# A decode step of attention and an MLP on one core: K tiles in pairs, two accumulator banks, and another order of the tail

## The chip, the core and the metric

The kernel runs on one core of one Trainium2 chip. The metric is the device time of one execution in microseconds, the median over runs. TensorE (PE; its weight loads PEld), VectorE (DVE), ScalarE (ACT) and GpSimd (POOL) compute; SyncE (SP) issues the large transfers, which the core's 16 DMA engines carry out in the order of issue.

## The reference, cut to what matters

Four tokens (B = 4) of width 576 go through an attention over a window of a cache and, in parallel, through a small MLP block; both are added to the input.

```python
xn = layernorm(x)                                   # x: 4 x 1 x 576
# A: attention, 32 query heads, 16 KV heads, Dh 128, window W = 2048 of the last keys of 8192
q = (xn @ wq) as 32 heads
k, v = the last 2048 rows of k_cache, v_cache, each KV head used by 2 query heads
A = (softmax(q k^T / sqrt(128)) v) as 4096 @ wo     # wo: 4096 x 576
# B: MLP; the shifts along the sequence leave zeros, since S = 1
x1 = xn + 0                                         # all four shifted groups are zero
B = x1 + gelu(layernorm(x1) @ w3) @ w4              # w3: 576 x 4608, w4: 4608 x 576
out = x + A + B
```

The time goes into moving data: K and V are 32 MB each in bf16, w3 and w4 5 MB each, wq and wo 4.6 MB each. That is 87 MB in all.

## The kernel before, in words

**Tiles.** K and V are read as eight tiles each of 4 MB (128 partitions x 32 KB), in an order K_order of (bp, kq): bp is a pair of batch elements (32 rows of batch and KV head each), kq is a quarter of the window. All go through one SBUF ring with four slots of a tile each; tile n lies in slot n % 4. Behind the four slots and partly over the last two lie wq and w3, later the first half of w4 (w4_e0, 18 rows of 576 per partition, at REST). The attention output weights wo and the second half of w4 (18 rows, in the pieces E1) come last, over slots 0 and 1.

**Transfers.** All of them are issued by SP, in program order, by cache_load (L124), load_run (L113) and load_w4 (L478). SP waits at each until the place in the ring is free: until VectorE has transposed the K tile there, or until TensorE's matmuls have read the V tile there. V0 to V3 come in two transfers of two tiles (64 KB per partition); K0 to K7 and V4 to V7 come one by one.

**K stage.** k_scores(n) (L278) issues the load of K tile n, lets VectorE transpose it in four instructions of 128 x 2048 int32 (L291) into kt tiles, of which there are two, and multiplies by the queries in 32 matmuls (L300). The scores stand in four PSUM banks S0 to S3. bank_max takes their maxima (L276).

**V stage.** From L508 on, TensorE, ScalarE and VectorE run in the order in which the program is written. exponentials(g) turn one bank into EP (L342). pick_rows (L348) turns the exponentials' rows by matmuls into the layout that V needs; ScalarE copies the result to CB (keep_rows, L358). spread_rows(n) (L367) makes the tile X(n) on VectorE in four instructions of 1.2 us (L373). X(n) is masked so that 64 matmuls of 128 x 256 (v_compute, L380) give the sums over V tile n, in the bank O0 (n = 0 to 3) or O1 (n = 4 to 7). X tiles share two buffers with the kt tiles, so X(n+1) takes the buffer of X(n-1). The matmuls of a quarter of a tile wait for the quarter of X alone.

**Heads.** reciprocal_rows (L394) brings 1 / sum to the rows where the heads are. heads_out(bp) (L405) scales the two halves of O. heads_rows (L410) turns them by four matmuls into OX, and heads_pick (L420) masks and sums OX on VectorE into onx, the left operand of the matmuls with wo. heads_out(0) follows v_compute(3), heads_pick(0) follows v_compute(4).

**The sum.** ACC is one PSUM bank: rows 0 to 3 hold columns 0 to 287 of the result, rows 32 to 35 hold columns 288 to 575. It is started with a matmul of zeros (L212), VectorE writes x + xn into it (L268), and acc_matmuls (L431) adds pairs of matmuls (4 x 288 each), one for each half. mlp_out adds rows of w4 in this way: 18 rows of w4_e0 in two halves, one behind v_compute(6), one behind heads_out(1). Then come the 32 rows of wo and the 18 rows of w4's second half. Last, ScalarE copies the one half of ACC and VectorE the other (L563), and the output is stored.

Of the kernel before, what the change touches and what calls it, by code (L numbers as in the profile page):

```python
# [9 lines left out]
ALU = mybir.AluOpType  # L10
AX = mybir.AxisListType
BF16 = mybir.dt.bfloat16
F32 = mybir.dt.float32
# [5 lines left out]
def kernel(  # L19
# [50 lines left out]
    def ap_of(t, offset_elems, dims):  # L70
        a = t[:]
        return bass.AP(a.tensor, a.offset + offset_elems, [list(a.ap[0])] + [list(d) for d in dims])
# [30 lines left out]
    w3_n = D * F // P  # L103
    wo_n = NQ * D // P
    E0_N = NFH * D
    E1 = (10, 6, 2)
    SLOT = [i * TILE for i in range(4)]
    REST = 4 * TILE
    RING = max(SLOT[2] + wq_n + w3_n, REST + E0_N)
# [11 lines left out]

    v_rows = A_v_cache.rearrange("b h s d -> (b h) s d")

    def cache_load(rows, n, count, tiles, paired):  # L124

        bp, kq = K_order[n]
        t = ring[:, SLOT[n % 4]:SLOT[n % 4] + count * TILE]
        lo = Sk - W + kq // 2 * 8 * CK
        src = rows[MT * bp:MT * bp + MT, lo:lo + 8 * CK, :]
        if paired:  # L130
            src = src.rearrange("m (q h c) d -> m q h (c d)", q=4, h=2)
        else:
            src = src.rearrange("m (h q c) d -> m q h (c d)", q=4, h=2)
        src = src[:, :, kq % 2:kq % 2 + count, :]
        load_run(t, src.rearrange("m q h x -> m q (h x)") if count > 1 else src[:, :, 0, :])
        for i in range(count):
            tiles[n + i] = t[:, i * TILE:(i + 1) * TILE].rearrange("p (c d) -> p c d", d=Dh)
# [40 lines left out]
    def z_part(n, dt):  # L178
        a = z_at[0]
        z_at[0] += n * (1 if dt is BF16 else 2)  # L180
        assert z_at[0] <= ZN
        return Z[:, a:a + n] if dt is BF16 else Zf[:, a // 2:a // 2 + n]
# [95 lines left out]
    def k_scores(n):  # L278

        bp, kq = K_order[n]  # L280
        cache_load(k_rows, n, 1, K_tiles, False)
        kn = K_tiles.pop(n)
        if n == 0:
            S.extend(ps_s.tile([P, 512], F32, tag="S", name=f"S{g}") for g in range(4))
        C2 = CK // 2

        kt = [ktp.tile([P, C2, G, 2, 2], BF16, tag="kt", name=f"kt{n}{e}") for e in range(2)]
        for i in range(4):
            e, a = divmod(i, 2)
            c0 = a * C2 // 2  # L290
            nc.vector.transpose(out=ap32(kt[e], c0 * 2 * G, [[2 * G, C2 // 2], [1, 2], [2, G]]),  # L291
                                in_=ap32(kn, c0 * 4 * G + e * G, [[4 * G, C2 // 2], [2 * G, 2], [1, G]]))
            if n > 4 and i == 1:
                bank_max(n - 5)
        for e in range(2):
            for t in range(2):
                y = 2 * e + t
                for m in range(NM):
                    c = 32 * (m % 4)
                    nc.tensor.matmul(out=S[kq][c:c + 32, :].rearrange("p (c q l) -> p c q l", q=4, l=2),  # L300
                                     lhsT=qz[:, bp, m, y, :], rhs=kt[e][:, :, 4 * m:4 * m + 4, :, t],
                                     start=(bp == 0 and m < 4 and y == 0), stop=(bp == 1 and m >= 4 and y == NY - 1),
                                     skip_group_check=True)
# [6 lines left out]
    permf = z_part(2 * 2 * PB, F32).rearrange("p (b s n) -> p b s n", b=2, s=2)  # L310
    osums = [z_part(Dh, F32) for bp in range(2)]
    masked = z_part(NT * 2 * Dh, F32).rearrange("p (t b x e) -> p t b x e", t=NT, b=2, x=XR)
    picked = z_part(NT * 2 * XR, F32)
    gu = z_part(NG2, F32)

    perm_rows = const.tile([P, 2, PB], BF16)
# [24 lines left out]
    def exponentials(g):  # L341
        nc.scalar.activation(out=EP[:, g].rearrange("p q (c l) -> p c q l", l=2),  # L342
                             in_=S[g][:].rearrange("p (c q l) -> p c q l", q=4, l=2),
                             func=ACT.Exp, bias=nb[:], scale=scale, accum_out=sm[:, g:g + 1])

    CPS = {}

    def pick_rows(bp, r, out, keys):  # L348
        for q in range(4):
            nc.tensor.matmul(out=out, lhsT=pick[:, bp, r, 3 - q:3 - q + P], rhs=ap_of(Z, q * 2 * CK, keys),  # L350
                             start=(q == 0), stop=(q == 3), skip_group_check=True)

    def pick_all(bp):
        for r in range(rep):
            CPS[bp, r] = ps_s.tile([P, NG * CK], F32, tag="S", name=f"C{bp}{r}")
            pick_rows(bp, r, CPS[bp, r][:], [[8 * CK, NG // 2], [1, 2 * CK]])

    def keep_rows(bp, g0, g1):  # L358
        for r in range(rep):
            nc.scalar.copy(out=CB[:, bp, g0:g1, :, r],  # L360
                           in_=CPS[bp, r][:, g0 * CK:g1 * CK].rearrange("p (g c) -> p g c", c=CK))
# [43 lines left out]
    def heads_out(bp):  # L405
        for j in range(2):
            rows = slice(PB * j, PB * j + PB)
            nc.scalar.mul(out=osums[bp][rows], in_=O_tiles[bp][rows, Dh * j:Dh * j + Dh], mul=rd_rows[rows, bp:bp + 1])

    def heads_rows(bp):  # L410
        OX = ps_tp.tile([P, NT, 2, Dh], F32, tag="tp", name=f"OX{bp}")
# [8 lines left out]
    def heads_pick(bp, OX):  # L420
        nc.vector.tensor_tensor(out=masked.rearrange("p t b x e -> p (t b) x e"),  # L421
                                in0=OX[:].rearrange("p t b (e x) -> p (t b) x e", x=XR),
                                in1=ap_of(own_d, 0, [[0, NT * 2], [0, XR], [1, ND]]), op=ALU.mult)
        nc.vector.tensor_reduce(out=picked, in_=masked.rearrange("p t b x e -> p (t b x) e"), op=ALU.add, axis=AX.X)  # L424
        nc.vector.tensor_copy(out=ap_of(onx, 2 * bp, [[XR * B, NT], [1, 2], [B, XR]]),  # L425
                              in_=picked.rearrange("p (t b x) -> p t b x", t=NT, b=2))

    def acc_rows(q):
        return slice(32 * q, 32 * q + B)

    def acc_matmuls(lhsT, row):  # L431
        for q in range(2):
            nc.tensor.matmul(out=ACC[acc_rows(q), 0:DH], lhsT=lhsT, rhs=row[:, q * DH:(q + 1) * DH],  # L433
                             start=False, stop=False, skip_group_check=True)

    G_banks = []
# [38 lines left out]
                             skip_group_check=True)  # L475
        nc.scalar.mul(out=gT[:], in_=GT[:], mul=0.5)

    def load_w4(a, e, i0, n):  # L478
        t = ring[:, a:a + n * D]
        nc.sync.dma_start(out=t, in_=w4_src[e, :, i0:i0 + n, :].rearrange("m i n -> m (i n)"))  # L480
        return t.rearrange("p (i n) -> p i n", n=D), e, i0, n


    def mlp_out(t, e, i0, n, a=0, b=None):
        for i in range(a, n if b is None else b):
# [13 lines left out]
    NV = len(K_order)  # L499
    w4_e0 = load_w4(REST, 0, 0, NFH)  # L500
    for n in range(0, 4, 2):
        cache_load(v_rows, n, 2, V_tiles, True)
    bank_max(NG - 1)
    nc.vector.reduce_max(out=nb[:], in_=mx[:], axis=AX.X)
    nc.vector.tensor_scalar_mul(out=nb[:], in0=nb[:], scalar1=-scale)  # L505
# [1 line left out]
    ENGINES = {mybir.EngineType.PE, mybir.EngineType.Activation, mybir.EngineType.DVE}  # L507
    with tc.manual_schedule(engines=ENGINES):  # L508
        exponentials(0)
        exponentials(1)  # L510
        first = ps_s.tile([P, rep, CK], F32, tag="S", name="first")
        for r in range(rep):
            pick_rows(0, r, first[:, r, :], [[1, CK]])
        exponentials(2)
        for r in range(rep):
            nc.scalar.copy(out=CB[:, 0, 0, :, r], in_=first[:, r, :])
        exponentials(3)
        spread_rows(0)
        v_compute(0, 0, CK // 2)
        pick_all(0)  # L520
        keep_rows(0, 1, NG)
        v_compute(0, CK // 2, CK)
        cache_load(v_rows, 4, 1, V_tiles, True)
        spread_rows(1)
        reciprocals()
        nc.scalar.copy(out=spread, in_=bass.AP(fold[:].tensor, fold[:].offset, [list(fold[:].ap[0]), [1, PB], [0, ND]]))
        for n in range(1, NV):
            v_compute(n)
            if n == 1:
                pick_all(1)  # L530
                keep_rows(1, 0, NG)
                reciprocal_rows()
            if n == 3:
                heads_out(0)
            if n + 1 < NV:
                spread_rows(n + 1)
            if n == 4:
                heads_pick(0, heads_rows(0))
                gelu_u()
            if n == 5:  # L540
                gelu_g()
                gelu_T()
            if n + 4 < NV:
                cache_load(v_rows, n + 4, 1, V_tiles, True)
            if n == 5:
                wo_t = load_run(ring[:, 0:wo_n], flat(A_wo, wo_n))
                end, i0 = [], 0
                for n1 in E1:
                    end.append(load_w4(wo_n + i0 * D, 1, i0, n1))
                    i0 += n1  # L550
            if n == 6:
                mlp_out(*w4_e0, 0, NFH // 2)
        heads_out(1)
        mlp_out(*w4_e0, NFH // 2, NFH)
        heads_pick(1, heads_rows(1))
        for x in range(XR):
            acc_matmuls(onx[:, 0, x, :], wo_t[:, x * D:(x + 1) * D])
        for part in end:
            mlp_out(*part)

    fin = const.tile([B, D], out.dtype, name="fin")
    for q, copy in enumerate((nc.scalar.copy, nc.vector.tensor_copy)):
        copy(out=fin[:, q * DH:(q + 1) * DH], in_=ACC[acc_rows(q), 0:DH])  # L563
    nc.scalar.dma_start(out=o2, in_=fin[:])


# [28 lines left out]
```

## Time and profile before

| What | us |
|---|---|
| median of the runs shown | 212.37 |
| runs | 286.46, 212.37, 212.02 |
| the profiled execution's own time | 212.37 |
| its span, first to last instruction | 210.3 |
| TensorE busy | 122.3 |
| VectorE busy | 128.1 |
| ScalarE busy | 14.6 |

The page divides the span in 40 equal slices of 5.26 us. "PEclk" gives the clock that TensorE was granted in each, in tenths of full speed; "DMA" the busy share of the 16 DMA engines. The chain that ended last follows the execution back from its last instruction: at each step to what released it, or to the instruction before it on its engine. A timeline's row gives start and duration of a group of merged instructions, then engine, line, operation, output and inputs, and in brackets how long the engine had been idle and what ended it ("issue" where the profile shows nothing). The time to landing of a transfer counts from its issue. K stands for the stretch to 121 us, V for the stretch from 131 us on.

### The profile page before, as it was taken

The page shows a single profiled execution, that of the slowest core. Times are in us where ns is not written, and L with a number is a line of the kernel's source. Part 1 is how long each engine was busy: PE and PEld are TensorE (multiplying, and loading weights), DVE is VectorE, ACT ScalarE, POOL GpSimd, SP SyncE. Part 2 cuts the span into 40 slices and gives each one's busy share as a digit, 9 for nine tenths or more (in the row PEclk, how much of TensorE's full clock was granted, in tenths as well). Part 3 has the DMA queues.
Part 4 walks back from the last instruction along what each step waited for, and adds up shares of the span by engine and source line. Part 5 has one row for each costly group of instructions (what it writes and reads, how often), then busy time and mean ns, then how long its engine had stood idle before and what let it go on. Part 6 is the DMA issues. An engine that isn't in the chain of part 4 may idle for free.

```text
span 210.3 us, 2423 instructions
## 1 busy us (share of the span) xinstructions
PE 122.3 (58%) x1071; PEld 75.9 (36%) x1071; DVE 128.1 (61%) x119; ACT 14.6 (7%) x40; POOL 3.2 (2%) x11
## 2 busy tenths in 40 slices
PE   1244199053534333333344400999799999799974
PEld 0121011010111111111111100778588889687752
DVE  6922100889898989899998180049935568950020
ACT  4002100000000000000000410020300101000100
POOL 4100000000000000000000000000000000000000
PEclk9999569855555555555555555599999999999999
DMA  7999999999999999999999999999999999999990
GB/s 300 399 452 465 392 427 461 405 430 461 405 430 461 397 411 474 411 424 461 400 501 399 436 424 511 411 411 402 405 418 452 424 418 433 443 425 438 386 378 25
DMA packets 3193, 87.31 MB, mean 415 GB/s; under 512 B 360, under 2 KB 368, under 8 KB 752
## 3 DMA queue, kind: packets, MB, share of 16 engines
q1 hardware_dynamic: 3168, 87.16, 96.6%
q8 instruction: 8, 0.13, 0.3%
q10 hardware_dynamic: 16, 0.01, 0.0%
q14 instruction: 1, 0.01, 0.0%
HBM read 87.17 MB, written 0.00 MB: 415 GB/s over the span
## 4 chain that ended last, share of the span: by engine, by line
DMA 52%; PE 31%; DVE 12%; issue 1%; SPq 1%; ACT 1%; DVEq 0%
DMA ring<-in_A_k_cache_dram 35%; PE O L386 25%; DMA ring<-in_A_v_cache_dram 17%; DVE kt L291 7%; PE ACC L433 4%; DVE X L373 2%; PE C L350 2%; SPq L114 1%; PE OX L416 1%; DVE Z L421 0%; DVE Z L424 0%; DVE Z L461 0%; DVE gg L465 0%; ACT Z L360 0%; DVE Z L460 0%
## 5 line engine op out<-in xcount | busy, mean ns | idle before, releaser
L291 DVE STREAM_TRANSPOSE kt<-ring 128x2048 int32<-128x2048 int32 x32 | 71.4, 2283 | 19.3 <-DMA ring<-in_A_k_cache_dram 19.2
L386 PE MATMUL O<-ring,X 128*128 128x256 bf16 x512 | 59.3, 279 | 10.6 <-DMA ring<-in_A_v_cache_dram 10.6
L300 PE MATMUL S<-kt,Z 128*32 128x512 bf16 x256 | 30.4, 623 | 50.0 <-DVE kt L291 50.0
L386 PEld LDWEIGHTS <-X 128*128 128x128 bf16 x512 | 51.1, 100 | 18.2 <-issue 11.1
L373 DVE TENSOR_TENSOR X<-Z,own 128x1024 int32<-128x1024 int32 x32 | 37.0, 1218 | 25.4 <-ACT Z L360 13.9
L300 PEld LDWEIGHTS <-Z 128*32 128x32 bf16 x256 | 10.2, 128 | 70.5 <-issue 70.5
L448 PE MATMUL G<-ring,ln2T 128*8 128x512 bf16 (+1 forms) x54 | 10.4, 859 | 2.6 <-DMA ring<-in_B_w_dram 2.6
L421 DVE TENSOR_TENSOR Z<-OX,own_d 128x256 f32<-128x256 f32 x2 | 0.8, 424 | 15.8 <-PE OX L416 15.8
L342 ACT ACTIVATE Z<-S,nb 128x512 bf16<-128x512 f32 x4 | 2.8, 700 | 81.0 <-DVE nb L505 81.0
L448 PEld LDWEIGHTS <-ln2T 128*8 128x8 bf16 x54 | 2.0, 98 | 12.3 <-issue 11.4
L229 PE MATMUL qp<-ring,xnT 128*8 128x512 bf16 x36 | 3.8, 578 | 2.3 <-DMA ring<-in_A_wq_dram 1.8
L240 DVE CAST q_rows<-qp 128x256 bf16<-128x256 f32 x4 | 1.5, 418 | 5.6 <-PE qp L229 4.9
L433 PE MATMUL ACC<-ring,gT 128*4 128x288 bf16 x72 | 4.9, 286 | 0.0
L433 PE MATMUL ACC<-ring,onx 128*4 128x288 bf16 x64 | 4.1, 286 | 1.2 <-DVE onx L425 1.2
L563 DVE CAST fin<-ACC 4x288 bf16<-4x288 f32 x1 | 0.4, 449 | 6.8 <-ACT fin L563 6.8
L360 ACT CAST Z<-C 128x384 bf16<-128x384 f32 (+1 forms) x4 | 2.6, 659 | 27.3 <-PE C L350 27.2
L350 PEld LDWEIGHTS <-pick 128*128 128x128 bf16 x24 | 2.4, 109 | 4.8 <-issue 3.3
L276 DVE TENSOR_REDUCE mx<-S 128x1 f32<-128x512 f32 x4 | 2.7, 671 | 2.0 <-PE S L300 2.0
L350 PE MATMUL C<-Z,pick 128*128 128x512 bf16 x16 | 3.8, 379 | 0.0
L196 PEld LDWEIGHTS <-Z 4*128 4x128 bf16 x16 | 0.8, 104 | 8.1 <-DVE Z L171 4.0
L433 PEld LDWEIGHTS <-onx 128*4 128x4 bf16 x64 | 2.7, 85 | 2.5 <-DVE onx L425 1.4
L433 PEld LDWEIGHTS <-gT 128*4 128x4 bf16 x72 | 3.0, 84 | 1.5 <-issue 0.4
(76 smaller groups left out, 41.9 us busy)
## 6 DMA issues: line engine op xcount, KB each, us to landing
ring<-in_A_k_cache_dram SPq DMA_DIRECT2D x8, 4096.0 KB, 32.5
ring<-in_A_v_cache_dram SPq DMA_DIRECT2D x4, 4096.0 KB, 21.0
ring<-in_B_w_dram SPq DMA_DIRECT2D x1, 5184.0 KB, 24.5
ring<-in_A_wo_dram SPq DMA_DIRECT2D x1, 4608.0 KB, 25.0
ring<-in_A_wq_dram SPq DMA_DIRECT2D x1, 4096.0 KB, 12.7
ring<-in_B_w_dram SPq DMA_DIRECT2D x1, 2592.0 KB, 35.5
ring<-in_B_w_dram SPq DMA_DIRECT2D x1, 1440.0 KB, 26.0
ring<-in_B_w_dram SPq DMA_DIRECT2D x1, 864.0 KB, 26.7
```

The lines of the kernel that those rows point to most:

```text
L114: nc.sync.dma_start(out=t, in_=src)
L229: nc.tensor.matmul(out=qp[32 * i:32 * i + 2 * B, :], lhsT=xnT[:, k:k + 2, :].rearrange("p e b -> p (e b)"), rhs=wq_t[:, f0:f0 + QN], start ...
L276: nc.vector.reduce_max(out=mx[:, g:g + 1], in_=S[g][:], axis=AX.X)
L291: nc.vector.transpose(out=ap32(kt[e], c0 * 2 * G, [[2 * G, C2 // 2], [1, 2], [2, G]]), in_=ap32(kn, c0 * 4 * G + e * G, [[4 * G, C2 // 2], ...
L300: nc.tensor.matmul(out=S[kq][c:c + 32, :].rearrange("p (c q l) -> p c q l", q=4, l=2), lhsT=qz[:, bp, m, y, :], rhs=kt[e][:, :, 4 * m:4 * ...
L342: nc.scalar.activation(out=EP[:, g].rearrange("p q (c l) -> p c q l", l=2), in_=S[g][:].rearrange("p (c q l) -> p c q l", q=4, l=2), func= ...
L350: nc.tensor.matmul(out=out, lhsT=pick[:, bp, r, 3 - q:3 - q + P], rhs=ap_of(Z, q * 2 * CK, keys), start=(q == 0), stop=(q == 3), skip_grou ...
L360: nc.scalar.copy(out=CB[:, bp, g0:g1, :, r], in_=CPS[bp, r][:, g0 * CK:g1 * CK].rearrange("p (g c) -> p g c", c=CK))
L373: nc.vector.tensor_tensor(out=ap32(X, a * CX * MT, [[MT, CX], [1, MT]]), in0=bass.AP(s32.tensor, s32.offset, [list(s32.ap[0]), [1, CX], [0 ...
L386: nc.tensor.matmul(out=O_tiles[bp][:], lhsT=X[:, c:c + 2, :].rearrange("p c n -> p (c n)"), rhs=vn[:, c:c + 2, :].rearrange("p c d -> p (c ...
L433: nc.tensor.matmul(out=ACC[acc_rows(q), 0:DH], lhsT=lhsT, rhs=row[:, q * DH:(q + 1) * DH], start=False, stop=False, skip_group_check=True)
L448: nc.tensor.matmul(out=G_banks[k][32 * c:32 * c + 2 * B, 0:n * P].rearrange("p (i m) -> p i m", m=P), lhsT=ln2T[:, NS - 1 - s:NS + 1 - s, ...
```

## The change

- E1 becomes (10, 4, 3, 1). The piece of 4 rows comes in two transfers of 64 partitions each.
- K0 to K3 come in two transfers of two tiles. For the first pair of batch elements (bp = 0), K and V tiles hold their keys in the arrangement of pairs; for the second, both in the arrangement of singles.
- The rows of EP that a V tile needs now lie in one bank of exponentials, so the first picks stand ahead of exponentials(1).
- reciprocal_rows moves from behind v_compute(1) to behind v_compute(2). With it a second bank ACC2 is made: a matmul of zeros, and a copy of rows 32 to 35 of ACC into it on VectorE. From then on the second half of the sum is added in ACC2.
- heads_out scales one half of O on ScalarE and the other on VectorE. heads_pick's reduction writes onx itself, and the copy behind it is gone.
- The 18 rows of w4_e0 all stand behind v_compute(7): six behind heads_out(1), twelve behind heads_rows(1).

```diff
-    E1 = (10, 6, 2)
+    E1 = (10, 4, 3, 1)
...
-    def cache_load(rows, n, count, tiles, paired):
+    def cache_load(rows, n, count, tiles):
...
-        if paired:
+        if bp == 0:
             src = src.rearrange("m (q h c) d -> m q h (c d)", q=4, h=2)
         else:
             src = src.rearrange("m (h q c) d -> m q h (c d)", q=4, h=2)
...
     def k_scores(n):
-        cache_load(k_rows, n, 1, K_tiles, False)
+        if bp or kq % 2 == 0:
+            cache_load(k_rows, n, 1 if bp else 2, K_tiles)
...
-    def pick_rows(bp, r, out, keys):
+    def pick_rows(bp, r, out, g0, g1):
         for q in range(4):
-            nc.tensor.matmul(out=out, lhsT=pick[:, bp, r, 3 - q:3 - q + P], rhs=ap_of(Z, q * 2 * CK, keys),
+            nc.tensor.matmul(out=out, lhsT=pick[:, bp, r, 3 - q:3 - q + P], rhs=EP[:, g0:g1, q, :],
                              start=(q == 0), stop=(q == 3), skip_group_check=True)
...
     def heads_out(bp):
         for j in range(2):
             rows = slice(PB * j, PB * j + PB)
-            nc.scalar.mul(out=osums[bp][rows], in_=O_tiles[bp][rows, Dh * j:Dh * j + Dh], mul=rd_rows[rows, bp:bp + 1])
+            src = O_tiles[bp][rows, Dh * j:Dh * j + Dh]
+            if j:
+                nc.vector.tensor_scalar_mul(out=osums[bp][rows], in0=src, scalar1=rd_rows[rows, bp:bp + 1])
+            else:
+                nc.scalar.mul(out=osums[bp][rows], in_=src, mul=rd_rows[rows, bp:bp + 1])
...
-        nc.vector.tensor_reduce(out=picked, in_=masked.rearrange("p t b x e -> p (t b x) e"), op=ALU.add, axis=AX.X)
-        nc.vector.tensor_copy(out=ap_of(onx, 2 * bp, [[XR * B, NT], [1, 2], [B, XR]]),
-                              in_=picked.rearrange("p (t b x) -> p t b x", t=NT, b=2))
+        with nc.allow_low_precision(reason="one term of each sum is not zero"):
+            nc.vector.tensor_reduce(out=ap_of(onx, 2 * bp, [[XR * B, NT], [1, 2], [B, XR]]),
+                                    in_=masked, op=ALU.add, axis=AX.X)
+
+    ACCS = [ACC]
...
         for q in range(2):
-            nc.tensor.matmul(out=ACC[acc_rows(q), 0:DH], lhsT=lhsT, rhs=row[:, q * DH:(q + 1) * DH],
+            nc.tensor.matmul(out=ACCS[q][acc_rows(q), 0:DH], lhsT=lhsT, rhs=row[:, q * DH:(q + 1) * DH],
                              start=False, stop=False, skip_group_check=True)
...
         exponentials(0)
-        exponentials(1)
         first = ps_s.tile([P, rep, CK], F32, tag="S", name="first")
         for r in range(rep):
-            pick_rows(0, r, first[:, r, :], [[1, CK]])
+            pick_rows(0, r, first[:, r, :], 0, 1)
+        exponentials(1)
         exponentials(2)
...
             if n == 1:
                 pick_all(1)
                 keep_rows(1, 0, NG)
+            if n == 2:
                 reciprocal_rows()
+                ACCS.append(ps_s.tile([P, 512], F32, tag="S", name="ACC2"))
+                nc.tensor.matmul(out=ACCS[1][:], lhsT=ident[:], rhs=zeros[:], start=True, stop=False, skip_group_check=True)
+                nc.vector.tensor_copy(out=ACCS[1][acc_rows(1), 0:DH], in_=ACC[acc_rows(1), 0:DH])
             if n == 3:
                 heads_out(0)
             if n + 1 < NV:
...
-                    end.append(load_w4(wo_n + i0 * D, 1, i0, n1))
+                    end.append(load_w4(wo_n + i0 * D, 1, i0, n1, (P // 2, P // 2) if n1 == E1[1] else (P,)))
                     i0 += n1
-            if n == 6:
-                mlp_out(*w4_e0, 0, NFH // 2)
         heads_out(1)
-        mlp_out(*w4_e0, NFH // 2, NFH)
-        heads_pick(1, heads_rows(1))
+        mlp_out(*w4_e0, 0, NFH // 3)
+        OX = heads_rows(1)
+        mlp_out(*w4_e0, NFH // 3, NFH)
+        heads_pick(1, OX)
...
-        copy(out=fin[:, q * DH:(q + 1) * DH], in_=ACC[acc_rows(q), 0:DH])
+        copy(out=fin[:, q * DH:(q + 1) * DH], in_=ACCS[q][acc_rows(q), 0:DH])
```

## The prediction, written before the changed kernel ran

> **What bounds the kernel now.** I read the page's slices first, then the chain that ended last, then the timelines of the second half engine by engine, then the transfers' times to landing. Times are microseconds from the span's start.
>
> ```profile
> PEclk9999569855555555555555555599999999999999
> DMA  7999999999999999999999999999999999999990
> ...
> q1 hardware_dynamic: 3168, 87.16, 96.6%
> ```
>
> The transfers run without a gap from the first slice to the last but one. A 4 MB tile lands every 9.72 in the trace, and the last piece of w4, issued at 179.59, lands 26.9 later, at 206.45. No order of the computation ends sooner than that. The chain shows who ends later still:
>
> ```profile
> 95.76 35.20 DMA ring<-in_A_v_cache_dram
> ...
> 131.09 6.07 PE O L386 x32
> ...
> 151.13 0.73 ACT Z L360
> 151.86 0.27 ACT Z L395
> ...
> 152.18 0.61 PE RD L399 x4
> 152.78 20.98 PE O L386 x192
> ...
> 181.49 0.74 DVE gg L465
> ...
> 190.76 7.09 PE O L386 x64
> ...
> 200.93 6.31 PE ACC L433 x100
> ...
> 207.27 0.40 ACT fin L563
> 207.69 0.45 DVE fin L563
> ```
>
> From the landing of the first V pair (130.96) to the end the chain stays on TensorE, with holes where it waits for ScalarE (151.1 to 152.2), VectorE's gg (181.2 to 182.3) and the head chain (199.7 to 200.9). So two limits run almost level: TensorE ends 0.8 behind the last transfer. A microsecond taken from TensorE alone is worth 0.8 at most; one added is paid whole. What feeds TensorE are the X tiles of VectorE (start, duration, instruction, idle time before it):
>
> ```profile
> 149.41 4.63 DVE L373 TENSOR_TENSOR X<-Z,own 128x1024 int32<-128x1024 int32 x4 [0.43 <-PE O L386]
> 159.89 4.63 DVE L373 TENSOR_TENSOR X<-Z,own 128x1024 int32<-128x1024 int32 x4 [5.84 <-issue]
> 166.81 4.63 DVE L373 TENSOR_TENSOR X<-Z,own 128x1024 int32<-128x1024 int32 x4 [2.30 <-PE O L386]
> ```
>
> These are X3, X4 and X5: each begins as soon as its buffer, that of the tile two before, is free, and so lies a whole 7.0 tile ahead of the matmuls that read it. That lead is what the change touches.
>
> **The change, part by part.** The profiled execution took 212.37, which is also the median of the runs shown: 210.26 of span and 2.11 around it.
>
> *Pairs of K tiles.* V comes in such pairs already: V2 and V3 land 19.36 after V0 and V1, where two singles take 19.44. So each K pair saves some 0.09, and the last landing goes from 206.45 to 206.27. The cost is at VectorE: K0 is usable at 46.95 with K1, not at 37.32. One K tile takes 8.85 there, 9.5 from K5 on with the maxima (L291, L276), so VectorE runs 47.1 to 64.8 for K0 and K1, waits for K2 and K3 (66.3), then goes through to 121.45, where before it ended at 115.02. SP's queue is held up by it: K4 goes out at 55.9, K5 at 64.8, K6 at 75.3, K7 at 84.1, the first V pair at 102.5, the second at 121.45. What is in flight by then drains no sooner than 64, 74, 84, 93, 109 and 129, so each issue is 6.5 to 9 ahead of need. Behind K7 the maximum, the exponentials and X0 follow as before, less some 0.25 because the first picks need one exponential instead of two. The first quarter of X0 (1.2) is ready at 128.4, and V0 lands at 130.8: 2.35 of cover, so nothing. V4 to V7 come in another order of the same 32 KB runs, in which K's singles land at the same 9.72: nothing.
>
> *reciprocal_rows moves behind v2.* v2 no longer waits for L360 and L395. It starts 0.2 behind the last pick, at 150.75 instead of 152.64 (V2 has landed at 150.15): -1.9.
>
> *The second bank.* Behind v2 TensorE runs the four RD matmuls (0.11 each) and one 128x512 matmul of zeros (L350 has 0.38 for that width at full clock; 0.59 at half clock is the other bound), ended at 158.6. Then VectorE copies a half of the sum. The row nearest is the 4x288 copy of L563, 0.45; bounds are 0.24 (L425) and 0.82 (L460). In the changed program's order this copy stands ahead of X3 on VectorE. So X3, which had begun at 149.41, begins at 159.1; its first quarter of 1.22 is done at 160.3, and v3 starts at 160.35, not at 158.4 where TensorE was free. A stall of 1.9.
>
> *The heads of the first half on two engines.* ScalarE's 64x128 scaling takes 0.36, 0.1 behind v3's end (167.5). VectorE's half of it has no row: between L425 (64 elements, 0.24) and L421 (256 elements from PSUM, 0.42) I take 0.30 for 128. It reads the same bank as ScalarE's, and as built it waits for ScalarE, as the two copies of L563 do above. It ends at 168.3, and again stands ahead of the next X: X4, at 159.89 before, begins at 168.3, its first quarter ends at 169.5, and v4 starts at 169.6 where TensorE was free at 167.35. A stall of 2.2. The Trainium skill ("PSUM — Partial Sum Buffer", "PSUM bank collisions raise a hardware error") says that two engines may be in one bank at once if their 32-partition quadrants differ. The two copies of L563 are in different quadrants (rows 0 and 32), and yet the trace has them one after the other; were the halves together, the sum would be lower by an estimated 0.3 or so.
>
> *Up to v7.* v5 follows v4 and OX0 at 177.0 (174.05 before). X5 ends on VectorE at 177.5, then come the pick of heads (0.43 and 0.42, the copy of 0.24 gone), gelu_u (1.6), X6 (4.6) and gg (0.8) to 185.4: TensorE waits 1.4 for gg, where it waited 1.25 before. v6 starts at 185.55 (182.42), and v7 directly behind it, the 18 matmuls of w4 between them gone (1.2): 192.55 to 199.7, against 197.85. wo's place in the ring is free at 178 (175.1); the queue drains no sooner than 187, so that is hidden.
>
> *The tail.* Behind v7 now stand 12 matmuls of w4 (0.0613 each), OX (0.6, from 200.55), 24 more, and then the 64 of wo from 202.5. VectorE's pick is done by 202.1 (202.4, if the reduction that writes onx takes 0.24 more), so the 1.2 that TensorE waited for it is filled. wo (199.9) and w4 (206.3 at the latest) have landed before their matmuls come: wo runs to 206.4, w4 to 208.78. Pieces of 4, 3 and 1 rows, and the halves of 64 partitions, cannot matter then: even at half the rate the 576 KB of the four rows end 1.4 later, ahead of the last matmuls.
>
> *The end.* The two fin copies no longer share a bank: 0.45 instead of 0.87. What follows keeps its 2.13.
>
> The sum: v2 earlier -1.9; RD and zeros behind v2 +0.65; the two stalls +1.9 and +2.2; gg +0.15; w4 out of the middle -1.2; the tail behind v7 -0.3; fin -0.4. That is +1.1: a span of 211.4, and **213.5** with the 2.11 around it. A measurement of this kernel tells about 2% (4.2) from no change, so this is within it.
>
> Uncertain is when the clock rises: at 136.08, 5.0 after v0 began; a rise one or two earlier or later moves v2 by half of that, and the V pair's landing stops it at -0.6. With the bounds of the copy (-0.2, +0.4) and of the other short rows (0.3 each way) the forecast's own range is 212.4 to 214.8.
>
> **The rivals.**
>
> *The transfers set the end.* If v7 is through by 197.6, 2.1 sooner than I have it, the last row of w4 ends the chain: 206.3, two matmuls (0.35 with the wait), fin 0.45 and 2.13 give a span of 209.25, and 211.35: faster than before. Without the two stalls v7 would end at 196. For it: the transfers are dense, and the tail is cleared of its waits. Against: in the built order both VectorE operations stand ahead of X3 and X4, and VectorE takes its queue in order.
>
> *The clock falls in the stalls.* The first row shows a stretch in which the clock was full and TensorE mostly idle, the second the next one, at half (columns: stretch, length, busy time and count of PE, PEld, DVE, ACT and POOL, granted clock, DMA share, GB/s):
>
> ```profile
> 16.61:20.03 3.42, 0.63 (x17) 0.13 (x6) 1.51 (x4) 1.20 (x4) 0.00 (x0) 1.00 0.90 388
> 20.03:30.27 10.24, 5.58 (x42) 1.53 (x42) 0.88 (x4) 0.93 (x5) 0.00 (x0) 0.50 0.95 412
> 131.09:136.08 4.99, 4.99 (x24) 3.58 (x25) 0.00 (x0) 0.00 (x0) 0.00 (x0) 0.50 1.15 499
> ```
>
> TensorE idled 2.8 of those 3.4 and lost the clock; the waits of 1.1 to 1.3 after 136 did not cost it. My stalls of 1.9 and 2.2 lie between. At half clock a V matmul took 0.213 instead of 0.109, so a fall for 3.4 costs 1.7: 215.2, and 216.9 for both stalls. The Trainium skill ("TensorE: Matmul & The Clock Gate", "What's actually happening") puts the fall behind at least one idle window of about 3.4; by that rule no stall here reaches it and the time stays at the forecast. The row above fell with a window not wholly idle, so the trace does not quite bear the rule out.
>
> *VectorE's late K tiles reach V.* This decides once VectorE is over 8.8 late instead of 6.4. If it makes up nothing, it is 9.7 late, X0 comes 0.95 behind V0, and the time is 214.5. Against: K2 to K7 run without a wait in my count, and the rows of L291 differ by less than 0.05.
>
> **How the numbers follow.** Forecast 0.62; transfers set the end 0.18 (whole or in part); clock 0.10; late K tiles 0.10. The time is the forecast's, 213.5. The range goes down to the first rival's 211.35, less 0.3 for the transfers' own rate, and up to one fall of the clock: 211.0 to 215.3. Faster by over 2% (below 208.1) would need an end before the transfers': 0.02. Slower by over 2% (above 216.6) is the clock falling twice, or a transfer queue run dry: 0.06. Within 2%: 0.92.
>
> **What would show it.** Right: X3 begins just behind the ACC2 copy near 159 and X4 behind the scaling near 168, with TensorE idle some 2 ahead of v3 and of v4; v7 ends near 199.7; the last transfer lands near 206.3, over 2 ahead of the last matmul; the fin copies overlap; VectorE's K tiles end near 121.5 and V0's matmuls still begin at 130.9. Wrong: X3 or X4 early, the last matmul right behind the last landing, half clock after 137, or V0's matmuls waiting for X0.

## The result and the profile after

The changed kernel took 214.62 (median of 214.28 to 215.51), the kernel before beside it 212.33. The ratio is 1.0119, 95% interval 1.0076 to 1.0162: slower by 1.2%, not faster, and within the 2% of the prediction. The forecast was 213.5, with 211.0 to 215.3 as its range. The ratio leaves out one slow execution of the kernel before (286.46). The profiled execution of the changed kernel is its longest, 215.51 with a span of 213.7.

First the slices of the changed kernel's page, to be laid beside those of before:

```profile
PEclk9999559555555555555555555699996999999999
DMA  7999999999999999999999999998999999999970
GB/s 295 399 439 497 445 396 392 552 417 392 405 392 460 417 391 472 405 411 472 408 549 396 405 429 393 527 405 383 423 399 457 417 460 420 399 437 438 352 196 1
```

The last row was this in the kernel before:

```profile
GB/s 300 399 452 465 392 427 461 405 430 461 405 430 461 397 411 474 411 424 461 400 501 399 436 424 511 411 411 402 405 418 452 424 418 433 443 425 438 386 378 25
```

Two things are new. The clock has a dent in the 31st slice (160 to 166). And the transfers still fill the span, but in the 38th and 39th slice they move 352 and 196 GB/s, where every slice from the second to the 37th moves 383 to 552, and where the kernel before had 386 and 378.

The chain that ended last (start, length, what) now runs through VectorE where the prediction put the two stalls:

```profile
151.55 6.99 PE O L386 x64
158.54 0.34 PE RD L399 x4
158.88 0.25 PE ACC L544
159.13 0.02 issue
159.15 0.46 DVE ACC L545
159.62 1.13 DVE X L373
160.75 0.05 issue
160.79 8.84 PE O L386 x64
...
169.72 0.37 ACT Z L412
170.09 0.03 issue
170.12 0.37 DVE Z L410
170.48 0.02 issue
170.50 9.17 DVE X L373 x8
...
203.34 7.74 PE ACC L439 x124
211.07 0.02 issue
211.10 0.45 DVE fin L576
```

The copy into ACC2 (L545) stands between TensorE and X3, the scaling of the half (L410) between v3 and X4. The waits in TensorE's timeline are 1.68 and 2.17 (forecast 1.9 and 2.2):

```profile
160.79 8.83 PE L386 MATMUL O<-ring,X 128*128 128x256 bf16 x64 [1.68 <-DVE X L373]
...
171.78 7.16 PE L386 MATMUL O<-ring,X 128*128 128x256 bf16 x64 [2.17 <-DVE X L373]
```

v3 itself takes 8.84 instead of 6.99, and a table of stretches along the clock's steps says why (stretch, length, busy time and count of PE, PEld, DVE, ACT and POOL, granted clock, DMA share, GB/s):

```profile
157.46:160.88 3.42, 1.74 (x16) 1.35 (x15) 1.73 (x3) 0.16 (x1) 0.00 (x0) 1.00 1.00 426
160.88:164.29 3.41, 3.41 (x17) 2.45 (x18) 3.26 (x3) 0.00 (x0) 0.00 (x0) 0.50 1.04 442
164.29:167.70 3.41, 3.41 (x33) 3.04 (x32) 0.00 (x0) 0.00 (x0) 0.00 (x0) 1.00 0.89 384
```

TensorE was busy for 1.74 of the 3.42 that end at 160.88; then its clock was 0.50 for 3.41, in which it did 17 matmuls instead of 33. The last piece of w4 shows in the list of transfers, issued at 185.62:

```profile
ring<-in_B_w_dram SPq DMA_DIRECT2D x1, 144.0 KB, 23.3
```

It lands at 208.95, not at 206.3. Here nobody waits for it: TensorE's 124 matmuls from 203.34 to 211.07 run through without a wait.

### The profile page after: what moved, and what is told of

Its sections match the earlier page's. It is cut to its first block, busy times and chain, and to the rows that moved or that the text cites. A ratio compares the mean times of both kernels' runs of the same rounds, so it can differ in the third digit from the quotient of the medians.

```text
span 213.7 us, 2415 instructions
## 1 busy us (share of the span) xinstructions
PE 124.4 (58%) x1071; PEld 76.9 (36%) x1072; DVE 127.8 (60%) x120; ACT 13.8 (6%) x38; POOL 3.2 (1%) x11
## 4 chain that ended last, share of the span: by engine, by line
PE 28%; DVE 16%; DMA 13%; issue 0%; ACT 0%; DVEq 0%; ACTq 0%
PE O L386 22%; DMA ring<-in_A_v_cache_dram 13%; DVE X L373 7%; DVE kt L292 6%; PE ACC L439 4%; PE C L350 2%; DVE Z L467 0%; DVE gg L471 0%; DVE Z L466 0%; PE OX L420 0%; DVE mx L276 0%; DVE ACC L545 0%; DVE fin L576 0%; DVE Z L425 0%; DVE onx L429 0%
## 5 line engine op out<-in xcount | busy, mean ns | idle before, releaser
L386 PE MATMUL O<-ring,X 128*128 128x256 bf16 x512 | 61.6, 285 | 8.9 <-DMA ring<-in_A_v_cache_dram 5.0
L386 PEld LDWEIGHTS <-X 128*128 128x128 bf16 x512 | 52.1, 102 | 18.1 <-DVE X L373 6.6
L410 DVE TENSOR_SCALAR Z<-O,rd_rows 64x128 f32<-64x128 f32 x2 | 0.7, 356 | 16.2 <-ACT Z L412 16.2
L545 DVE COPY ACC<-ACC 4x288 f32<-4x288 f32 x1 | 0.5, 462 | 9.7 <-PE ACC L544 9.7
```

What stands on the lines that cost most here:

```text
L386: nc.tensor.matmul(out=O_tiles[bp][:], lhsT=X[:, c:c + 2, :].rearrange("p c n -> p (c n)"), rhs=vn[:, c:c + 2, :].rearrange("p c d -> p (c ...
```

## The experiments

**One copy moved.** Theory A: the two VectorE operations ahead of X3 and X4 cost the time. Theory B: the halves of 64 partitions slow the end of the transfers.

```diff
-                nc.vector.tensor_copy(out=ACCS[1][acc_rows(1), 0:DH], in_=ACC[acc_rows(1), 0:DH])
...
             if n + 1 < NV:
                 spread_rows(n + 1)
+            if n == 2:
+                nc.vector.tensor_copy(out=ACCS[1][acc_rows(1), 0:DH], in_=ACC[acc_rows(1), 0:DH])
```

> The changed kernel with one line moved: VectorE's copy into ACC2 stands behind X3 instead of ahead of it. Theory A (the two VectorE operations ahead of X3 and X4 are what costs): X3 begins near 149.8 again, v3 starts where the matmul of zeros ends (159.1), no fall of the clock there, and TensorE is 1.7 earlier for the stall and another 1.7 where the clock fell; the stall of 2 ahead of v4 stays. TensorE alone would end near 207.5, a time of 212.2. Theory B (the 64-partition halves of w4's four rows slow the last transfers, which landed at 208.95 instead of 206.3): the last landing stays near 208.9 and now sets the end, 214.0. If neither holds, 214.6 as the changed kernel.

213.52 (213.32 to 214.29), ratio 1.0067 (1.0044 to 1.0090). TensorE's timeline:

```profile
158.37 7.15 PE L386 MATMUL O<-ring,X 128*128 128x256 bf16 x64
167.69 7.16 PE L386 MATMUL O<-ring,X 128*128 128x256 bf16 x64 [2.17 <-DVE X L373]
...
207.50 0.66 PE L439 MATMUL ACC<-ring,gT 128*4 128x288 bf16 x8 [1.08 <-DMA ring<-in_B_w_dram]
208.42 0.66 PE L439 MATMUL ACC<-ring,gT 128*4 128x288 bf16 x8 [0.26 <-DMA ring<-in_B_w_dram]
```

The stall ahead of v3 is gone and the one ahead of v4 is as before. TensorE now waits for w4 at the end: with one stall taken away, the transfers set it. Both theories hold their part.

**Both moved.** The scaling of O0's second half goes behind spread_rows(4) as well (heads_out(0, (0,)) ahead of it, heads_out(0, (1,)) behind it).

> The changed kernel with both VectorE operations moved behind the X tile that they delayed: the copy into ACC2 behind X3, the scaling of O0's second half behind X4. Theory A alone: no stall ahead of v3 and v4, v7 through near 196, and the transfers set the end: 211.3. Theory B with it: the stalls are gone as well, but w4 lands near 208.9 and the time stays near 214.0, TensorE waiting for the last pieces. A rival to both (the clock alone, or the new bank): 214 with TensorE still idle ahead of v3 or v4.

214.03 (213.40 to 214.65), ratio 1.0095 (1.0058 to 1.0132). v3 and v4 follow v2 without a wait (the first row), and nothing is won: TensorE waits at each piece of w4.

```profile
158.34 14.13 PE L386 MATMUL O<-ring,X 128*128 128x256 bf16 x128
...
204.73 1.39 PE L439 MATMUL ACC<-ring,gT 128*4 128x288 bf16 x20 [0.76 <-DMA ring<-in_B_w_dram]
207.27 0.66 PE L439 MATMUL ACC<-ring,gT 128*4 128x288 bf16 x8 [1.14 <-DMA ring<-in_B_w_dram]
208.27 0.66 PE L439 MATMUL ACC<-ring,gT 128*4 128x288 bf16 x8 [0.35 <-DMA ring<-in_B_w_dram]
```

**And the four rows in one transfer.**

```diff
-                    end.append(load_w4(wo_n + i0 * D, 1, i0, n1, (P // 2, P // 2) if n1 == E1[1] else (P,)))
+                    end.append(load_w4(wo_n + i0 * D, 1, i0, n1))
```

> As the run before it, and the four rows of w4 come in one transfer of 128 partitions instead of two of 64. Theories A and B together: the last landing is back near 206.3 and the time is 211.3, below the kernel before. If the halves are not what slows the end of the transfers: the same as the run before it.

211.33 (211.13 to 211.51), ratio 0.9960 (0.9948 to 0.9972). This beats both kernels. The last landing is at 206.25, and the timeline of its end has the two fin copies together:

```profile
205.97 0.66 PE L439 MATMUL ACC<-ring,gT 128*4 128x288 bf16 x8 [0.23 <-DMA ring<-in_B_w_dram]
...
206.66 0.39 ACT L579 CAST fin<-ACC 4x288 bf16<-4x288 f32 x1 [10.11 <-PE ACC L439]
206.69 0.45 DVE L579 CAST fin<-ACC 4x288 bf16<-4x288 f32 x1 [8.06 <-PE ACC L439]
```

**The pieces alone, in the kernel before.** E1 = (10, 4, 3, 1) and load_w4 with its parts, nothing else of the change.

> The kernel before with one part of the change alone: w4's second half in pieces of 10, 4, 3 and 1 rows, the four rows in two transfers of 64 partitions. Theory B: the last landing moves from 206.45 to 209, TensorE waits for it, and the time goes from 212.3 to 214.4. Theory A alone (the pieces cost nothing): 212.4, the last row's two matmuls 0.3 behind the landing at 206.5.

214.48 (214.30 to 214.68), ratio 1.0106 (1.0083 to 1.0130): theory B to 0.1. The timeline has the wait that did not exist before:

```profile
207.95 0.66 PE L433 MATMUL ACC<-ring,gT 128*4 128x288 bf16 x8 [1.55 <-DMA ring<-in_B_w_dram]
208.87 0.66 PE L433 MATMUL ACC<-ring,gT 128*4 128x288 bf16 x8 [0.26 <-DMA ring<-in_B_w_dram]
```

**The changed kernel with the four rows whole.** The diff is that of the third run, on the changed kernel.

> The changed kernel with one part undone: the four rows of w4 in one transfer of 128 partitions. Theory A (the stalls ahead of v3 and v4 set the end of the changed kernel, the slow transfers are hidden behind them): the last landing goes back to 206.3 and TensorE's last matmul does not move: near 209.3 without a fall of the clock, a time of 214.0, and 215.5 in an execution where the clock falls for one window. Rival (the slow transfers set the end and the stalls are hidden): 211.5.

Six executions: 212.84, 212.85, 214.17, 214.49, 214.63, 214.94; ratio 1.0087 (1.0055 to 1.0119). The last landing is back (206.91, in an execution whose transfers all ran 0.6 later), and TensorE's end did not follow it (its last 36 matmuls start at 208.00 and run through): the stalls alone set this kernel's end. The median, 214.33, is 0.3 below the changed kernel's, within the scatter of both. The times fall in two groups. The profiled execution, 214.94, has its fall of the clock behind the other stall:

```profile
166.62:170.03 3.41, 1.25 (x12) 0.88 (x11) 1.93 (x3) 0.36 (x1) 0.00 (x0) 1.00 0.98 423
170.03:173.44 3.41, 3.41 (x18) 2.43 (x17) 3.41 (x4) 0.00 (x0) 0.00 (x0) 0.50 1.05 452
```

**The stalls filled.**

```diff
                 nc.tensor.matmul(out=ACCS[1][:], lhsT=ident[:], rhs=zeros[:], start=True, stop=False, skip_group_check=True)
+                idle = ps_s.tile([P, 512], F32, tag="S", name="idle")
+                for _ in range(8):
+                    nc.tensor.matmul(out=idle[:], lhsT=ident[:], rhs=zeros[:], start=True, stop=True, skip_group_check=True)
...
             if n == 3:
+                for _ in range(9):
+                    nc.tensor.matmul(out=idle[:], lhsT=ident[:], rhs=zeros[:], start=True, stop=True, skip_group_check=True)
                 heads_out(0)
```

> As the run before it, with matmuls of zeros into an unused bank put where TensorE stands still: 8 ahead of v3, 9 ahead of v4 (0.216 each). v3 and v4 begin as before, TensorE is busy meanwhile. If an idle stretch of 1.7 to 2.2 is what took the clock from the changed kernel's profiled execution: the clock stays full from 137 on in this one and the times stand close together near 214.0, with none at 215.5. If the fall has another cause (a window's phase alone, v3's matmuls): falls as before.

212.81 (212.68 to 212.88, seven executions), ratio 1.0031 (1.0020 to 1.0042). The timeline shows v3 and v4 as late as with the stalls (they begin 9.40 and 18.73 behind v2's begin, 9.41 and 18.73 in the run before it), with the zeros (L547, L551) ahead of them:

```profile
157.80 1.89 PE L547 MATMUL idle<-zeros,ident 128*128 128x512 bf16 x8
159.64 7.16 PE L386 MATMUL O<-ring,X 128*128 128x256 bf16 x64
166.64 2.11 PE L551 MATMUL idle<-zeros,ident 128*128 128x512 bf16 x9
168.97 7.16 PE L386 MATMUL O<-ring,X 128*128 128x256 bf16 x64 [0.22 <-DVE X L373]
```

The clock stayed full from 134.37 to the end, the mean granted clock is 0.773 or 0.774 in all seven, and the upper group of times is gone. So the idle time, not the lateness, takes the clock; by the two groups of the run before it costs 1.3 to 2.1. The 214.0 that I expected without a fall was 1.2 too high: I had worked it from the changed kernel's profiled execution, in which v2 began at 151.39; here it began at 150.24.

**What about the halves is slow.** Three forms of the kernel with both operations moved: two transfers of two rows each on 128 partitions, four transfers of 32 partitions, and two of 64 that take every second partition (in this order in the diff).

```diff
+            src = w4_src[e, :, i0 + r0:i0 + r0 + step, :].rearrange("m i n -> m (i n)")
...
-                    end.append(load_w4(wo_n + i0 * D, 1, i0, n1, (P // 2, P // 2) if n1 == E1[1] else (P,)))
+                    end.append(load_w4(wo_n + i0 * D, 1, i0, n1, (P // 4,) * 4 if n1 == E1[1] else (P,)))
...
+            src = w4_src[e, p0:P:step, i0:i0 + n, :].rearrange("m i n -> m (i n)")
+            nc.sync.dma_start(out=t[p0:P:step], in_=src)
```

> The kernel with both VectorE operations behind their X tiles, and the four rows of w4 in two transfers again, but each of 128 partitions and two rows. If 64 partitions are what slows a transfer: the last landing is near 206.3 and the time 211.4, as with one transfer. If it is one more transfer: landing near 208.6 and 214.0.

> The same kernel with the four rows in four transfers of 32 partitions. If the rate of a transfer goes with its partitions (64 partitions: packets of 4608 bytes took 0.31 instead of 0.18): these packets take some 0.6 to 0.7 and the last landing comes 3 to 6 behind that of the halves, the time 217 to 220. If halves and quarters cost the same: 214.

> The kernel with both VectorE operations behind their X tiles, and the four rows of w4 in two transfers of 64 partitions, but every second partition instead of one half and then the other. Theory C (a DMA engine that keeps to the 8 neighbouring partitions that it writes in a transfer of 128 goes at full rate; in the halves two engines write the same 8 at once): packets of 4608 bytes take 0.18 again, the last landing is near 206.4 and the time 211.4. If it is that a transfer has 64 partitions, wherever they lie: 0.31, 208.6 and 214.0, as the halves.

| four rows of w4 | packet of the rows, median | last landing | time | ratio (95%) |
|---|---|---|---|---|
| one transfer | 0.180 (4608 B) | 206.25 | 211.33 | 0.9960 (0.9948 to 0.9972) |
| two, by rows | 0.094 (2304 B) | 206.43 | 211.35 | 0.9963 (0.9950 to 0.9976) |
| two, every second partition | 0.179 (4608 B) | 206.49 | 211.38 | 0.9961 (0.9945 to 0.9978) |
| two halves of 64 partitions | 0.307 (4608 B) | 208.56 | 214.03 | 1.0095 (1.0058 to 1.0132) |
| four quarters of 32 | 0.309 (4608 B) | 208.59 | 214.07 | 1.0092 (1.0073 to 1.0111) |

Packets and landing are those of the profiled execution, the time is the median. With halves and with quarters the executions stand in two pairs (213.40 and 213.51, 214.55 and 214.65; 213.69 and 213.71, 214.43 and 214.58), and the profiled one is of the lower pair; what parts the pairs no trace shows.

It is neither one more transfer nor 64 partitions as such, but where they lie. Neighbours are slow, a spread over all 128 is not. Why is not shown. Theory C fits the interleaved run, but which partitions a DMA engine writes is in no trace, and neither it nor the rate theory has quarters cost no more than halves. A reading that fits all five rows is a limit that belongs to the block of partitions and not to the engine: a quarter would reach as much of it as the half that it lies in (0.309 and 0.307), and a spread over 128 all of it. A run with 64 neighbours from partition 32 on, across both halves, would put it to the test; there is none.

**What the other parts bring.** From the third run's kernel, K0 to K3 in singles again (first), and one bank for the sum again (second).

```diff
-        if bp or kq % 2 == 0:
-            cache_load(k_rows, n, 1 if bp else 2, K_tiles)
+        cache_load(k_rows, n, 1, K_tiles)
...
-    ACCS = [ACC]
+    ACCS = [ACC, ACC]
...
```

> The kernel with both VectorE operations behind their X tiles and the four rows of w4 in one transfer (211.33), with one part of the change undone: K0 to K3 in four transfers of 32 KB per partition, in the same arrangement of keys. The transfers set the end there, so a saving of 0.09 for each pair shows: the last landing near 206.45 and 211.5. If the pairs save nothing at the end: 211.3. VectorE's K tiles end near 115 again, which changes nothing by either.

> The same kernel with another part undone: one bank for both halves of the sum, without the matmul of zeros and the copy. Of 211.33, the two fin copies stand one behind the other again: +0.42, 211.75. If the copies' order doesn't matter: 211.3.

Singles: 211.35 (211.27 to 211.69), last landing 206.45, against 211.33 and 206.25 with pairs. Neither tells the two apart: other kernels with pairs and the four rows whole land their last piece at 206.28 (stalls filled), 206.36 (one bank) and 206.91. Whether the pairs save the expected 0.09 each stays open. One bank: 211.63, ratio 0.9970 (0.9959 to 0.9980); the fin copies begin at 206.77 and 207.19, one behind the other. The second bank brings 0.3 of the expected 0.42.

## Why the prediction was right, and where it was wrong

**The order on VectorE: right.** The copy held X3 to 159.53 (forecast 159.1), the scaling held X4 to 170.50 (168.3; 1.8 of the difference is the fall of the clock in v3). Without both operations in the way, and the transfers mended, the time is 211.33, which is the first rival's 211.35.

**The rival of the clock: underrated.** It had 0.10, and 215.2. It came in the profiled execution, which took 215.5. For the other three there is no trace, but a run lists its span and its mean granted clock, and span x 2 x (1 - clock) is the time at half clock. That is 99.0 in the executions of 214.28 and 214.31. With the four rows whole it is 98.9 in the traced execution with its fall, and 99.0 and 99.1 in two more of the upper four. In 99 executions of the other kernels it is 95.4 to 97.9 or at least 102.4, never between. So the fall very likely came in at least three of the changed kernel's four executions; 214.92 cannot be told in this way.

The Trainium skill ("TensorE: Matmul & The Clock Gate", "What's actually happening") has the half rate after at least one idle window of some 3.4. The traces differ: the clock fell at the end of windows that were idle for 49% (the changed kernel) and 63% (the four rows whole). In the run with the one copy moved, a stall of 2.17 lay across two windows of 3.4, 32% and 31% idle, and the clock stayed. Within each trace the clock's steps lie whole multiples of 3.41 apart, but not at the same place in the program: it rose at 136.99 in the changed kernel's profiled execution and at 134.37 in the filled one's. A reading that fits is that it depends on how a stall of 1.7 to 2.2 falls on these windows, so that one kernel has executions with and without the fall; no run tested it by itself.

**The pieces of w4: wrong.** "Pieces of 4, 3 and 1 rows, and the halves of 64 partitions, cannot matter then: even at half the rate the 576 KB of the four rows end 1.4 later." The term was too small. The last piece lands 2.3 to 2.7 later, because transfers beside the halves are slowed too: packets of the ten rows ahead took up to 0.84, where none took over 0.44 without halves, and those of the three rows behind took 0.23 instead of 0.14. Alone the pieces cost the kernel before 2.4. In the changed kernel's profiled execution they cost nothing: TensorE ends at 211.03, 2.1 behind the landing, and 1.8 of that is the fall. Without a fall TensorE is through at 208.2 (the filled kernel), not at the 208.8 that I took as cover, and the halves and quarters land at 208.6 to 209.1 in the five traces that have them. So they would set the end there. That one of the changed kernel's four executions was of this kind is not shown.

**The sum, and some luck.** For the profiled execution: 211.4 forecast, +0.6 because the clock rose at 136.99 and v2 began at 151.39 (an allowance of half a microsecond to one was named for that), +1.8 for the fall. That is 213.8, measured 213.7. What stands around the span is 1.8 and not 2.11; why is open. With the stalls and without a fall or halves the time is 212.8 (the lower two with the four rows whole, and the filled kernel), 0.7 below the forecast: 0.4 in the span (211.0; v2 began at 150.24, not 150.75) and 0.3 around it. With 1.3 to 2.1 for a fall that gives 214.1 to 214.9, and the median, 214.62, lies there, 1.1 above the forecast. So the two stalls were rightly foreseen, but that the median is no further off is partly luck: a sum 0.7 too high met a loss that was not in it.

**What was costed at nothing: right.** VectorE's K tiles ended at 121.08 (121.45), X0's first quarter was done at 128.0, and v0 began with V0's landing, at 131.12. SP's later issues of K and V left the DMA row at 9 tenths but for one slice at 8 (144 to 150). The halves of heads_out ran one behind the other (169.72 and 170.12), VectorE's in 0.36 instead of the 0.30 that I took; VectorE's waits there for ScalarE's, so no run tells whether they could lie together. The fin copies overlap (211.06 and 211.10).

## What to carry to other kernels

In an engine whose queue is in order, the place of a small operation counts, not its length: a copy of 0.46 that waited for the end of v2, ahead of a tile that had some 9 of lead, cost 1.7, and the same copy behind that tile cost TensorE nothing. Where two limits run level, take both away before a part is judged: here each of two losses hid the other (without the stalls 214.03, without the halves 214.33, without both 211.33). A last transfer that is cut should, by these runs, be cut along the rows of every partition, not into blocks of partitions.

## What the runs showed of the hardware that was not expected

- A transfer to 64 or 32 neighbouring partitions moves packets of 4608 bytes in 0.31 instead of 0.18; to every second partition of 128, in 0.18. The Trainium skill ("DMA: Bandwidth & Descriptors", "Why a DMA increments its semaphore by 16 and not by 1") has a transfer of 64 partitions on as many engines as one of 128, and each half did count 16 completions. By that it is not the number of engines that differs; which engine wrote where the traces do not show.
- A window of 3.41 that is half idle can be enough for the clock to fall: 49% and 63% idle did it, 44% (the second stall of the changed kernel) did not. Both falls lasted 3.41.
- Matmuls of zeros into an unused bank, where TensorE would stand still, kept the clock up: 212.68 to 212.88 with them, 212.84 to 214.94 without.
